# Linear attention and a mixture of adapters on one core: one order of tokens up to the store, x added by several engines, a tangent for the last slots

## The chip, the core and the metric

The kernel runs on one core of a Trainium2 chip. A core has five engines that run their own instruction streams: TensorE (PE, matrix products and transposes into PSUM), VectorE (DVE), ScalarE (ACT), GpSimd (POOL, which has no access to PSUM) and SyncE (SP, used here to issue transfers). Sixteen DMA engines move data between DRAM and the on-chip memory SBUF. An engine works through its stream in order and waits on semaphores for the work of others.

The metric is the time of one execution on the device in microseconds, lower is better.

## The reference

Two stages follow each other. The first is linear attention with cosine weights on q, k, v of shape (8, 8, 576, 64): batch, heads, positions, head size. Each relu'd row is taken twice, times the cosine and times the sine of its position's angle.

```python
    def phi(x, c, s):
        r = np.maximum(x, 0.0)
        return np.concatenate([r * c, r * s], axis=-1)
    q_p = phi(q, cos_w, sin_w)
    k_p = phi(k, cos_w, sin_w)
    kv = np.einsum('bhsf,bhsd->bhfd', k_p, v)
    z = np.sum(k_p, axis=2)
    num = np.einsum('bhsf,bhfd->bhsd', q_p, kv)
    den = np.einsum('bhsf,bhf->bhs', q_p, z)[..., None] + 1e-06
    return (num / den).astype(np.float32)
```

Its result, with the heads side by side, is x: 4608 tokens (8 batches of 576) of 512 numbers. The second stage adds a mixture of eight low-rank adapters: a gate chooses two experts per token, and

```python
    logits = x @ w_gate
    ...
            z = x[mask] @ A[e]
            delta[mask] += w[mask, k, None] * (z @ B[e])
    return (x + delta).astype(np.float32)
```

The output is 4608 x 512 in fp32, 9.44 MB; q, k and v are 9.44 MB each.

## The kernel before

**Tiles.** The 576 positions of a batch are written as 64 rows r of 9 positions s, position = 9 r + s. A batch's q, k and v are loaded with partition = (head parity, r), 128 of them, and cast to bf16 on the way (fp32 for batch 0's k and v). A **slot** n (0 to 35) is 128 tokens: two values of s, with 64 rows each. In the tokens of a slot the number j of the s comes first, then r: token = 64 j + r. Slots 4, 13, 22 and 31 are mixed: they take s = 8 of two neighbouring batches. Nine slots make two batches.

**Steps of a batch.** `ldv`, `ldk`, `ldq` load (batch 0's v and k by SP, all others by POOL's queue). `vs` multiplies one s of v by a cosine (i = 0) or a sine (i = 1), on ACT, DVE or POOL; `rk` and `qc` apply relu to k and q; `kv` sums the products of k and v in PSUM, and `kve` copies them out.

**Steps of a slot.** `qt` transposes q; `qe` multiplies it, read from PSUM, by the table `tabq` of cosines and sines into `qT`: 8 columns of 128, half for each table. `nd` gives numerator and denominator (the small constant of the denominator comes in by a product of `ones` and `eps_hi`); `re` and `no` divide, which gives x as a bf16 tile; `xt` and `xe` transpose x; `za` gives the adapters' z and the gate's logits.

**Steps of a group** (three slots, at the end two and one). `mx`, `nm`, `mk`, `tt`, `cb`, `sg` choose the experts and their weights, `zg` weighs z, `zt` transposes it into PSUM, and `ze` copies it to SBUF. Then, for each slot, `dx` (lines 439 and 440) makes the output in PSUM with two products: `turn` times x, and z times B. `oe` copies it into one of 22 output tiles, and `st` stores it.

**Order of tokens.** `turn` is a permutation matrix (line 483): the first product of `dx` adds x and brings its tokens from (j, r) into (r, j). `ze` permutes z in the same way (lines 421 to 423). So the output tile has partition = 2 r + j, and the store walks DRAM as r, j, d:

```python
        t = out.rearrange("(x r s) d -> x s r d", s=NS, r=HALF)
        dst = t[b:b + 2, s] if mixed(n) else t[b, s:s + 2]
        ...
        e.dma_start(out=dst[:, :, c].rearrange("j r d -> r j d"), in_=o_t[n % NO][:, c])
```

One piece is 2 KB, the 512 numbers of a token; a store has 128 of them, 256 KB.

**What sets the order.** The text `ORDER` lists every step with its engine (T, A, V, G or W for POOL, S); each engine's stream is its steps in that order, and no scheduler moves them. W is a POOL step that in addition waits for DVE's last `vs`, `rk` or `qc`. Buffers set waits too: slot n's `oe` takes the tile that slot n - 22 stored from, and most output tiles lie in the memory of batches whose k and v are used up. SP's stream is five loads at the start, then `gate`, then all 36 stores. `gate` (line 219) is a pair of transfers of two elements each: the first reads v of batch 7, and so waits until that load has landed, and the second waits for the first. No store is issued before that.

Of the kernel before, what the change touches and what calls it, by code (L numbers as in the profile page):

```python
# [21 lines left out]
ldv,S,0,0 pre,G start,A ldk,S,0,0 ldw,S ldq,G,0,0 tq,A ldv,G,1,0 ldk,G,1,0 ldq,G,1,0 ldv,G,2,0 vs,A,0,3,0  # L22
vs,V,0,5,1 ldk,G,2,0 cols,V vs,A,0,4,1 vs,V,0,7,1 vs,A,0,5,0 kz,G,1 kz,V,2 vs,A,0,8,0 vs,A,0,8,1 vs,A,0,1,0
vs,V,0,4,0 vs,A,0,7,0 kz,V,0 vs,A,0,0,1 vs,A,0,2,1 vs,A,0,0,0 vs,V,0,6,0 vs,A,0,1,1 vs,A,0,3,1 rk,V,0,0 rk,A,0,1
vs,V,0,2,0 vs,V,0,6,1 kv,T,0,0 qc,V,0,1 kv,T,0,1 qc,V,0,0 kv,T,0,2 qt,T,1 kve,A,0,0 qt,T,0 kve,A,0,1 qe,V,0
cw,A,0 qe,V,1 dm,T,n0 dm,T,n0 dm,T,n0 nd,T,0 qt,T,3 re,V,0 qt,T,2 no,V,0 qe,V,3 vs,G,1,8,0 vs,A,1,3,1 dm,T,b0
dm,T,b0 nd,T,1 vs,A,1,5,0 vs,G,1,6,1 vs,V,1,2,0 xt,T,0 vs,A,1,6,0 vs,W,1,7,1 xe,A,0 re,V,1 qe,V,2 vs,G,1,5,1
vs,A,1,8,1 vs,G,1,0,1 no,V,1 vs,A,1,2,1 ldq,G,2,0 vs,A,1,4,1 vs,V,1,1,1 dm,T,b0 dm,T,b0 dm,T,b0 dm,T,b0 dm,T,b0
dm,T,b0 nd,T,2 vs,V,1,1,0 vs,A,1,0,0 rk,V,1,0 ldv,G,3,0 xt,T,1 vs,A,1,7,0 xe,A,1 vs,V,1,4,0 ldk,G,3,0 dm,T,b0
kv,T,1,0 vs,V,1,3,0 re,V,2 za,T,0 no,V,2 ldq,G,3,0 kv,T,1,1 mx,V,0 nd,T,3 qc,V,1,0 xt,T,2 kv,T,1,2 re,V,3  # L30
qc,V,1,1 xe,A,2 za,T,1 no,V,3 kve,A,1,1 qt,T,4 qt,T,5 kve,A,1,0 za,T,2 qe,V,4 xt,T,3 mx,V,1 xe,A,3 mx,V,2 nd,T,4
qe,V,5 vs,W,2,5,1 vs,A,2,2,0 nm,V,0 mk,V,0 qt,T,6 vs,A,2,8,0 tt,V,0 ldv,G,4,0 re,V,4 cb,V,0 no,V,4 sg,A,0
vs,A,2,2,1 ldk,G,4,0 zg,V,0 cw,A,1 xt,T,4 qt,T,7 qe,V,6 vs,G,2,1,0 vs,A,2,0,1 zt,T,0 nd,T,5 vs,G,2,6,0 ze,A,0
qe,V,7 za,T,3 xe,A,4 vs,G,2,5,0 dx,T,1,b0 re,V,5 mx,V,3 vs,A,2,6,1 vs,G,2,7,0 no,V,5 dx,T,0,b1 vs,A,2,0,0
vs,G,2,4,0 qt,T,8 rk,V,2,0 oe,A,0 nd,T,6 ldq,G,4,0 oe,A,1 xt,T,5 qe,V,8 za,T,4 vs,W,2,1,1 xe,A,5 re,V,6
vs,G,2,3,1 vs,A,2,3,0 mx,V,4 kv,T,2,0 no,V,6 ldv,G,5,0 vs,A,2,7,1 za,T,5 qc,V,2,1 vs,A,2,4,1 nd,T,7 mx,V,5
vs,A,2,8,1 qc,V,2,0 xt,T,6 mk,V,1 kv,T,2,1 nm,V,1 re,V,7 xe,A,6 tt,V,1 cb,V,1 no,V,7 kv,T,2,2 sg,A,1 qt,T,9
zg,V,1 kve,A,2,0 nd,T,8 vs,W,3,0,1 qe,V,9 kve,A,2,1 vs,G,3,0,0 xt,T,7 zt,T,1 qt,T,10 vs,G,3,5,0 re,V,8 za,T,6
ze,A,1 no,V,8 qt,T,11 vs,G,3,5,1 xe,A,7 dx,T,2,b0 qe,V,10 vs,G,3,1,1 nd,T,9 oe,A,2 vs,G,3,2,1 qe,V,11 xt,T,8
vs,A,3,2,0 vs,G,3,8,1 za,T,7 dx,T,3,b1 re,V,9 xe,A,8 ldq,G,5,0 mx,V,7 no,V,9 dx,T,4,b0 vs,A,3,1,0 za,T,8  # L40
rk,V,3,0 vs,G,3,6,1 nd,T,10 oe,A,4 oe,A,3 xt,T,9 mx,V,6 mx,V,8 qt,T,12 re,V,10 vs,W,3,4,1 nm,V,2 vs,A,3,3,0
mk,V,2 no,V,10 kv,T,3,0 vs,G,3,3,1 vs,A,3,4,0 qe,V,12 vs,G,3,7,0 xe,A,9 nd,T,11 vs,G,3,8,0 vs,A,3,7,1 tt,V,2
qc,V,3,1 kv,T,3,1 ldk,G,5,0 vs,A,3,6,0 re,V,11 xt,T,10 cb,V,2 qc,V,3,0 kv,T,3,2 sg,A,2 ldv,G,6,0 xe,A,10 no,V,11
qt,T,13 kve,A,3,1 qt,T,14 zg,V,2 ldk,G,6,0 nd,T,12 vs,A,4,1,0 qe,V,14 xt,T,11 kve,A,3,0 vs,W,4,6,1 zt,T,2 za,T,9
qe,V,13 ldv,G,7,0 xe,A,11 za,T,10 re,V,12 dx,T,5,b0 ze,A,2 no,V,12 vs,G,4,8,1 vs,A,4,3,1 za,T,11 dx,T,6,b1
vs,G,4,5,0 vs,A,4,0,0 mx,V,10 mx,V,9 mx,V,11 nd,T,13 vs,G,4,3,0 nm,V,3 oe,A,6 rk,V,4,0 vs,W,4,2,1 oe,A,5 xt,T,12
mk,V,3 qt,T,16 re,V,13 tt,V,3 qt,T,15 vs,G,4,1,1 xe,A,12 no,V,13 dx,T,7,b1 vs,G,4,7,0 vs,A,4,0,1 dx,T,8,b0
cb,V,3 qe,V,15 vs,G,4,5,1 sg,A,3 nd,T,14 oe,A,7 vs,G,4,4,0 zg,V,3 xt,T,13 oe,A,8 vs,G,4,2,0 qt,T,17 re,V,14
zt,T,3 no,V,14 za,T,12 vs,A,4,6,0 vs,G,4,4,1 kv,T,4,0 xe,A,13 mx,V,12 vs,G,4,7,1 qe,V,16 nd,T,15 vs,A,4,8,0
ldq,G,6,0 qc,V,4,0 xt,T,14 kv,T,4,1 re,V,15 qc,V,4,1 xe,A,14 za,T,13 no,V,15 ze,A,3 kv,T,4,2 vs,W,5,5,0  # L50
vs,A,5,1,1 qe,V,17 za,T,14 vs,G,5,2,0 kve,A,4,0 nd,T,16 mx,V,13 mx,V,14 vs,G,5,5,1 kve,A,4,1 xt,T,15 mk,V,4
nm,V,4 qt,T,19 re,V,16 vs,G,5,2,1 tt,V,4 qt,T,18 xe,A,15 no,V,16 dx,T,10,b0 vs,G,5,7,0 vs,A,5,0,0 cb,V,4
dx,T,9,b1 qe,V,18 vs,G,5,3,1 sg,A,4 nd,T,17 vs,G,5,6,0 oe,A,10 zg,V,4 qt,T,20 vs,G,5,0,1 oe,A,9 xt,T,16 re,V,17
zt,T,4 no,V,17 vs,G,5,7,1 za,T,15 dx,T,11,b0 xe,A,16 vs,G,5,3,0 mx,V,15 qe,V,19 nd,T,18 ze,A,4 vs,G,5,4,0
oe,A,11 qc,V,5,0 xt,T,17 vs,G,5,1,0 za,T,16 re,V,18 qe,V,20 xe,A,17 dx,T,12,b1 vs,W,5,6,1 dx,T,13,b0 ldk,G,7,0
no,V,18 qt,T,21 za,T,17 oe,A,12 rk,V,5,0 vs,W,5,8,0 nd,T,19 oe,A,13 xt,T,18 mx,V,17 qc,V,5,1 vs,A,5,4,1
vs,W,5,8,1 kv,T,5,0 mx,V,16 nm,V,5 qt,T,22 mk,V,5 re,V,19 tt,V,5 kv,T,5,1 no,V,19 vs,G,6,2,1 vs,A,6,5,1 xe,A,18
# [466 lines left out]
```

## Time and profile before

| | |
|---|---|
| median of 3 runs | 105.99 us (105.93 to 106.36) |
| the profiled execution | 105.92 us |
| its span, first to last instruction | 104.1 us |
| PE, DVE, ACT, POOL busy | 91.0, 87.3, 82.3, 57.3 us |
| mean granted clock of PE | 0.997 |
| moved by the DMA engines | 25.55 MB in 19225 packets |
| HBM read, written | 28.85 MB, 9.44 MB |

The time contains the span and 1.8 us around it. The page gives the span in 40 slices of 2.6 us; "GB/s" is what the DMA engines wrote in a slice. The loads that cast read two bytes for each one they write, so their figure is half of what is read. Queue q0 holds POOL's transfers, q1 those of SP, q10 that of ACT. A busy PE is not a PE at its peak, since matmuls are pipelined and their ends are modelled.

### The profile page before, as it was taken

The numbers are of one execution on the slowest core, as the hardware profiler recorded it, in microseconds if no ns is written. First come the engines' busy times: TensorE is split into PE (matmuls) and PEld (weight loads), VectorE is DVE, ScalarE is ACT, GpSimd is POOL, SyncE is SP. The second block draws the span as 40 slices with busy tenths as digits, with TensorE's granted clock in tenths as the row PEclk, the third lists the DMA queues.
The fourth block names the chain that finished last, engine by engine and source line by source line (L and its number), as shares of the span: only waits on it lengthen the run. The fifth ranks groups of instructions, "written<-read, shape, count | busy, mean of one in ns | idle before, by whom it ended". The sixth has DMA issues, their size and how long they took to land.

```text
span 104.1 us, 3984 instructions
## 1 busy us (share of the span) xinstructions
PE 91.0 (87%) x1620; PEld 65.7 (63%) x1620; DVE 87.3 (84%) x264; ACT 82.3 (79%) x176; POOL 57.3 (55%) x112
## 2 busy tenths in 40 slices
PE   4999489879794999999999999999999999998810
PEld 1344267457573887867887789688778677665200
DVE  5058769579995999999999999999999999999710
ACT  6969767918899699999899789979984896967820
POOL 6991004960799696997979869998910000000000
PEclk9999999999999999999999999999999999999998
DMA  2999999999999999999999999999999996989992
GB/s 27 364 358 291 216 208 247 208 207 213 203 208 213 204 206 210 208 213 204 208 210 205 208 207 207 210 206 126 188 397 372 349 334 257 376 307 383 381 384 96
DMA packets 19225, 25.55 MB, mean 245 GB/s; under 512 B 2184, under 2 KB 13448, under 8 KB 19208
## 3 DMA queue, kind: packets, MB, share of 16 engines
q0 software_dynamic: 11616, 12.98, 73.8%
q1 hardware_dynamic: 7064, 12.21, 32.8%
q8 instruction: 12, 0.20, 0.7%
q10 hardware_dynamic: 528, 0.13, 0.6%
q14 instruction: 5, 0.04, 0.1%
HBM read 28.85 MB, written 9.44 MB: 368 GB/s over the span
## 4 chain that ended last, share of the span: by engine, by line
PE 53%; DMA 18%; ACT 11%; POOL 9%; issue 2%; DVE 2%; POOLq 0%; ACTq 0%
DMA q<-in_q_dram 18%; PE nd L324 10%; PE big L258 8%; PE xz L349 6%; PE za L358 6%; PE big L439 6%; PE big L440 5%; PE pq L289 5%; POOL vs L244 4%; ACT xT L353 3%; ACT zgT L423 2%; PE nd L313 2%; POOL q L200 2%; PE xz L415 2%; POOL k L200 1%
## 5 line engine op out<-in xcount | busy, mean ns | idle before, releaser
L244 POOL TENSOR_SCALAR vs<-v,tab 128x256 bf16<-128x256 bf16 x78 | 37.9, 501 | 17.8 <-DMA v<-in_v_dram 8.7
L353 ACT COPY xT<-xz 128x512 bf16<-128x512 bf16 x34 | 20.0, 587 | 8.9 <-PE xz L349 8.3
L297 DVE TENSOR_TENSOR qT<-pq,tabq 128x1024 bf16<-128x1024 bf16 x36 | 23.8, 676 | 0.9 <-PE pq L289 0.8
L243 ACT ACTIVATE vs<-v,tab 128x256 bf16<-128x256 bf16 x43 | 20.0, 512 | 0.9 <-DMA v<-in_v_dram 0.6
L343 DVE TENSOR_TENSOR xt<-nd,rden 128x512 bf16<-128x512 f32 x28 | 19.2, 687 | 0.3
L324 PE MATMUL nd<-kvsb,qT 128*128 128x130 bf16 (+1 forms) x256 | 19.1, 221 | 0.4 <-DVE qT L297 0.4
L258 PE MATMUL big<-vs,k 64*64 64x130 bf16 x576 | 12.4, 221 | 4.3 <-DVE k L251 2.7
L324 PEld LDWEIGHTS <-qT 128*128 128x128 bf16 (+1 forms) x256 | 13.6, 100 | 2.9 <-issue 1.1
L349 PE MATMUL xz<-ident,xt 128*128 128x128 bf16 x144 | 14.1, 220 | 1.2 <-DVE xt L343 0.7
L358 PE MATMUL za<-AW,xT 128*128 128x136 bf16 x144 | 14.4, 223 | 0.1
L258 PEld LDWEIGHTS <-k 64*64 64x64 bf16 x576 | 9.2, 106 | 7.2 <-DVE k L251 3.5
L289 PE MATMUL pq<-ident,qq 128*128 128x128 bf16 x144 | 13.0, 219 | 0.2 <-DVE qq L282 0.2
L439 PE MATMUL big<-xt,turn 128*128 128x512 bf16 x31 | 11.7, 378 | 0.4 <-ACT k L444 0.3
L349 PEld LDWEIGHTS <-xt 128*128 128x128 bf16 x144 | 10.2, 114 | 2.6 <-DVE xt L343 0.9
L440 PE MATMUL big<-Ball,zgT 128*128 128x512 bf16 x31 | 11.8, 380 | 0.0
L468 PE MATMUL nd<-ones 128*128 128x512 bf16 x36 | 9.4, 427 | 1.5 <-DVE eps_hi L469 1.5
L275 ACT CAST kvsb<-big 64x520 bf16<-64x520 f32 x16 | 9.5, 593 | 1.5 <-PE big L258 1.1
L358 PEld LDWEIGHTS <-xT 128*128 128x128 bf16 x144 | 9.4, 98 | 1.9 <-ACT xT L353 0.8
L289 PEld LDWEIGHTS <-qq 128*128 128x128 bf16 x144 | 9.2, 98 | 1.9 <-DVE qq L282 0.3
L319 PE MATMUL nd<-eps_hi,ones 128*128 128x4 bf16 x56 | 9.5, 169 | 0.1
L282 DVE TENSOR_SCALAR qq<-q 128x1152 bf16<-128x1152 bf16 x16 | 8.1, 513 | 0.8 <-DMA q<-in_q_dram 0.8
L468 PEld LDWEIGHTS <-ones 128*128 128x128 bf16 x36 | 3.8, 108 | 6.6 <-issue 1.9
(81 smaller groups left out, 148.1 us busy)
## 6 DMA issues: line engine op xcount, KB each, us to landing
q<-in_q_dram POOLq DMA_DIRECT2D x8, 576.0 KB, 17.1
v<-in_v_dram POOLq DMA_DIRECT2D x7, 576.0 KB, 17.6
k<-in_k_dram POOLq DMA_DIRECT2D x7, 576.0 KB, 17.0
out_dram<-k SPq DMA_DIRECT2D x10, 256.0 KB, 4.2
out_dram<-v0f SPq DMA_DIRECT2D x8, 256.0 KB, 4.5
out_dram<-k0f SPq DMA_DIRECT2D x8, 256.0 KB, 3.8
out_dram<-v SPq DMA_DIRECT2D x6, 256.0 KB, 3.3
v0f<-in_v_dram SPq DMA_DIRECT2D x1, 1152.0 KB, 5.5
```

The costliest lines, as they stand in the source:

```text
L243: return e.activation(dst, src, AF.Copy, bias=0.0, scale=t)
L244: return e.tensor_scalar(out=dst, in0=src, scalar1=t, scalar2=1.0, op0=ALU.mult, op1=ALU.mult)
L258: e.matmul(out=big[halves[g2], par, gp * 2 * W:(gp + 1) * 2 * W], lhsT=k_b[b][pr, 2 * gp + g2, s, :], rhs=vs_t[b % NV][pr, s, 2 * gp + g2, ...
L289: e.transpose(out=d[:, gp, :, jj, :], in_=q2_t[b % 3][:, gp, s].rearrange("p g d -> p (g d)"), identity=ident)
L297: e.tensor_tensor(out=qT_t[n % NQ], in0=src, in1=tab, op=ALU.mult)
L324: e.matmul(out=nd[pr, par, gp * 2 * W:(gp + 1) * 2 * W], lhsT=qT[:, i, gp * 2 + par, js], rhs=kv_t[b % 3][:, par, gp, i, :], start=False, ...
L343: e.tensor_tensor(out=x.rearrange("p (a t d) -> p t a d", t=2, d=D), in0=nds()[:, :, :, 0:D], in1=rd.rearrange("p (t a) -> p t a", t=2).to ...
L349: e.transpose(out=xz[:, c * 128:(c + 1) * 128], in_=x[:, c], identity=ident)
L353: (e.copy if e is nc.scalar else e.tensor_copy)(xT_t[n % 3], src)
L358: e.matmul(out=zs[:, i, :], lhsT=xT_t[n % 3][:, c, :], rhs=AW[:, c, :], start=(c == 0 and i == 0), stop=(c == DCH - 1), skip_group_check=True)
L439: e.matmul(out=d, lhsT=turn, rhs=x_t[n % NX], start=True, stop=False)
L440: e.matmul(out=d, lhsT=zgT_t[g % 3][:, n - GROUPS[g][0], :], rhs=Ball, start=False, stop=True)
```

## The change

- **One order of tokens.** `turn` is gone, `dx` uses the identity, `ze` is a plain copy (on DVE for groups 8 and 12). Output tiles have partition = 64 j + r, and the store walks DRAM as j, r, d.
- **x added by any engine.** A text `ADD` says for each slot who adds x: PE as before (0), `oe` on DVE (1, slot 30), or a new step `ox` on POOL, which adds x to the output tile after `oe` has copied it (2, twelve slots: 3, 12, 16 to 19, 21, 23 to 27). In slots of kinds 1 and 2 `dx` is one product, z times B.
- **Slots 26 on.** `qT` holds q itself and q times the tangent, in place of q times cosine and sine; numerator and denominator are then both too large by 1/cosine, and the small constant is divided by the cosine as well. The plain half is a copy on ACT (`qe,A,n,0`; slot 27's on DVE), the other a product with the table `tanq` on DVE (`qe,V,n,1`). `ones` is replaced by `esec` in the constant's product for these slots. The table is now kept for pairs of s; tables in fp32 are made first, and `tc`, `tn`, `te`, `tl` derive the bf16 ones, the tangent and `esec` from them.
- **A new ORDER** with these steps. Per engine the counts change thus: `vs` ACT 55 to 65, POOL 78 to 73, DVE 11 to 6; warming matmuls `dm` 12 to 11; all else is as listed above. On POOL's queue the loads keep their order, but for v of batch 7, which goes ahead of k of batch 6 (18th of 22 instead of 19th), and several are issued earlier among POOL's other work, q of batch 7 directly behind k of batch 7. The stores have an order of their own: slots 13, 3, 10, 1, 2, 0, 6, 11, 16, 20, 9, 15, 5, 4, 12, 7, 18, 17, 21, 19, 8, 22, 14, 23, 26, 24, 28, 25, 29, 27, 32, 31, 30, 33, 34, 35.

The core of the diff (`ORDER` left out):

```diff
-    turn = sb("turn", [128, 128])
...
+    NP = NS // 2 + 1
+    posq = sb("posq", [128, NP, 128], mybir.dt.int32)
+    cosq = sb("cosq", [128, NP, 128], FP32)
+    sinq = sb("sinq", [128, NP, 128], FP32)
+    tabq = sb("tabq", [128, 2, NP, 128])
+    tanq = sb("tanq", [128, NP, 128])
+    esec = sb("esec", [128, NP, 128])
...
+ADD = "000200000000200022220202222200100000"
...
+    def tc_(e):
+        copy = e.copy if e is nc.scalar else e.tensor_copy
+        copy(tabq[:, 0], cosq)
+        copy(tabq[:, 1], sinq)
+
+    def tn(e):
+        e.reciprocal(cosq, cosq)
+        e.tensor_tensor(out=tanq, in0=sinq, in1=cosq, op=ALU.mult)
+
+    def te(e):
+        e.activation(esec, cosq, AF.Copy, bias=0.0, scale=EPS)
+
+    def tl(e):
+
+        for pr in (slice(32, 64), slice(96, 128)):
+            e.scalar_tensor_tensor(out=esec[pr], in0=cosq[pr], scalar=EPS, in1=esec[pr],
+                                   op0=ALU.mult, op1=ALU.subtract)
...
-    def qe(e, n):
...
+    def qe(e, n, i=None):
+
+        p, dst = tokens(n)[0][1] // 2, qT_t[n % NQ]
+        src = pq[n % 2][:, 0:512].rearrange("p (a t) -> p a t", a=4)
+        if i is None:
+            src = src.unsqueeze(1).broadcast_to([128, 2, 4, 128])
+            tab = tabq[:, :, p].unsqueeze(2).broadcast_to([128, 2, 4, 128])
+        else:
+            dst = dst[:, i]
+            tab = tanq[:, p].unsqueeze(1).broadcast_to([128, 4, 128])
+        if i == 0:
+            return (e.copy if e is nc.scalar else e.tensor_copy)(dst, src)
+        e.tensor_tensor(out=dst, in0=src, in1=tab, op=ALU.mult)
...
-        e.matmul(out=d, lhsT=turn, rhs=x_t[n % NX], start=True, stop=False)
-        e.matmul(out=d, lhsT=zgT_t[g % 3][:, n - GROUPS[g][0], :], rhs=Ball, start=False, stop=True)
+        by_pe = ADD[n] == "0"
+        if by_pe:
+            e.matmul(out=d, lhsT=ident, rhs=x_t[n % NX], start=True, stop=False)
+        e.matmul(out=d, lhsT=zgT_t[g % 3][:, n - GROUPS[g][0], :], rhs=Ball, start=not by_pe, stop=True)
 
     def oe(e, n, h=None):
...
+        if ADD[n] == "1":
+            return e.tensor_tensor(out=d, in0=s, in1=x_t[n % NX], op=ALU.add)
         (e.copy if e is nc.scalar else e.tensor_copy)(d, s)
+
+    def ox(e, n):
+        return e.tensor_tensor(out=o_t[n % NO], in0=o_t[n % NO], in1=x_t[n % NX], op=ALU.add)
 
     def st(e, n, h=None):
         (b, s), _ = tokens(n)
         t = out.rearrange("(x r s) d -> x s r d", s=NS, r=HALF)
         dst = t[b:b + 2, s] if mixed(n) else t[b, s:s + 2]
         c = slice(0, DM) if h is None else slice(h * DM // 2, (h + 1) * DM // 2)
-        e.dma_start(out=dst[:, :, c].rearrange("j r d -> r j d"), in_=o_t[n % NO][:, c])
+
+        e.dma_start(out=dst[:, :, c], in_=o_t[n % NO][:, c])
```

More of the change, by code (lines that the diff above doesn't have):

```diff
@@ L85 @@
+dx,T,33,b1 sg,A,12 st,S,30 dx,T,34,q1 zg,V,12 oe,A,33 zt,T,12 oe,A,34 ze,V,12 st,S,33 dx,T,35,b0 st,S,34 oe,A,35
+st,S,35
 """
@@ L107, in by_rows, with by_tan @@
     return n >= ROWS and not mixed(n)
+def by_tan(n):
+    return n >= TANS
 @with_exitstack
@@ L305, in nd_ @@
             for g2, pr in enumerate(halves):
-                e.matmul(out=nd[:, g2, D:4 * W:W], lhsT=ones[pr, 0:128], rhs=eps_hi2[pr], start=True,
+                e.matmul(out=nd[:, g2, D:4 * W:W], lhsT=el[pr], rhs=r4[pr], start=True,
                          stop=False, skip_group_check=True)
@@ L318, in nd_ @@
         for par in range(2):
-            e.matmul(out=nd[:, par, D:4 * W:W], lhsT=ones[:, 0:128], rhs=eps_hi, start=True,
+            e.matmul(out=nd[:, par, D:4 * W:W], lhsT=el, rhs=r2, start=True,
                      stop=False, skip_group_check=True)
@@ L433, in dx @@
             for i in range(2):
-                e.matmul(out=h[i], lhsT=turn, rhs=x_t[n % NX][:, i * DM // 2:(i + 1) * DM // 2], start=True, stop=False)
+                e.matmul(out=h[i], lhsT=ident, rhs=x_t[n % NX][:, i * DM // 2:(i + 1) * DM // 2], start=True, stop=False)
             for i in range(2):
```

166 lines of the change are left out of this document (83 added, 83 removed).

## The prediction

> **What bounds the kernel now.** I read the page first: busy shares, then the slices of the transfer rate. In the second fence the columns are start, end, length and the busy time of each engine, then the granted clock, the busy share of the 16 DMA engines (above 1 because packets overlap) and GB/s.
>
> ```profile
> span 104.1 us, 3984 instructions
> PE 91.0 (87%) x1620; PEld 65.7 (63%) x1620; DVE 87.3 (84%) x264; ACT 82.3 (79%) x176; POOL 57.3 (55%) x112
> GB/s 27 364 358 291 216 208 247 208 207 213 203 208 213 204 206 210 208 213 204 208 210 205 208 207 207 210 206 126 188 397 372 349 334 257 376 307 383 381 384 96
> ```
>
> ```profile
> 60.00:70.00 10.00, 9.93 (x235) 8.03 (x234) 9.75 (x31) 8.94 (x21) 9.27 (x20) 1.00 1.21 208
> 70.00:75.00 5.00, 5.00 (x89) 4.08 (x87) 5.00 (x15) 4.71 (x11) 4.56 (x8) 1.00 1.05 152
> 75.00:80.00 5.00, 4.87 (x127) 3.86 (x126) 4.96 (x17) 3.68 (x9) 0.94 (x3) 1.00 1.06 378
> 85.00:90.00 5.00, 5.00 (x93) 3.52 (x92) 4.77 (x16) 3.84 (x9) 0.00 (x0) 1.00 0.80 295
> 95.00:100.00 5.00, 3.83 (x23) 1.48 (x21) 3.50 (x12) 3.44 (x8) 0.00 (x0) 1.00 1.03 383
> 100.00:104.10 4.10, 0.00 (x0) 0.00 (x0) 0.00 (x0) 0.00 (x0) 0.00 (x0) 0.92 0.54 201
> ```
>
> The transfers never rest. From about 18 us to 70 the loads hold a flat 203 to 213 GB/s; from 75 us the stores run at up to 383. DVE (9.75 of 10) and PE (9.93) are full as well, so loads and arithmetic advance side by side, and the last ten microseconds are a queue of stores drained at full rate: 24.6 us of stores (9.44 MB at 383) fit between 75 and 102. So the shape of a store bears on the end directly. When stores may begin is in the SP queue, and what carries them in the page's part on queues and in the list of issues:
>
> ```profile
> 66.37 0.75 SPq L221 DMA_DIRECT2D gone<-v  x1
> 70.85 0.58 SPq L222 DMA_DIRECT2D gone<-gone  x1
> 71.55 0.67 SPq L451 DMA_DIRECT2D out_dram<-v0f  x1
> ```
>
> ```profile
> q0 software_dynamic: 11616, 12.98, 73.8%
> q1 hardware_dynamic: 7064, 12.21, 32.8%
> q10 hardware_dynamic: 528, 0.13, 0.6%
> ...
> q<-in_q_dram POOLq DMA_DIRECT2D x8, 576.0 KB, 17.1
> v<-in_v_dram POOLq DMA_DIRECT2D x7, 576.0 KB, 17.6
> k<-in_k_dram POOLq DMA_DIRECT2D x7, 576.0 KB, 17.0
> out_dram<-k SPq DMA_DIRECT2D x10, 256.0 KB, 4.2
> out_dram<-v0f SPq DMA_DIRECT2D x8, 256.0 KB, 4.5
> out_dram<-k0f SPq DMA_DIRECT2D x8, 256.0 KB, 3.8
> out_dram<-v SPq DMA_DIRECT2D x6, 256.0 KB, 3.3
> v0f<-in_v_dram SPq DMA_DIRECT2D x1, 1152.0 KB, 5.5
> k0f<-in_k_dram SPq DMA_DIRECT2D x1, 1152.0 KB, 10.3
> out_dram<-osb SPq DMA_DIRECT2D x4, 256.0 KB, 4.1
> Bf<-in_moe_B_dram SPq DMA_DIRECT2D x1, 256.0 KB, 15.5
> ...
> Af<-in_moe_A_dram SPq DMA_DIRECT2D x1, 128.0 KB, 13.4
> Wf<-in_moe_w_gate_dram SPq DMA_DIRECT2D x1, 16.0 KB, 13.6
> gone<-v SPq DMA_DIRECT2D x1, 0.0 KB
> gone<-gone SPq DMA_DIRECT2D x1, 0.0 KB
> ```
>
> The packet counts say how many engines carry a transfer. A load on q0 is 128 partitions by 4 runs, 512 pieces; 22 loads make 11264, and 11616 leaves 352, which is 22 times 16: sixteen closing packets for each. On q10 one transfer of 512 pieces leaves 16. On q1 the pieces are 2 x 512 (v0f, k0f), 512 (Af), 128 (Wf), 128 (Bf), 36 x 128 (stores) and 2 x 2 (the two-element gate, an element a piece): 6404. That leaves 660. Forty-one transfers with an outer count of 128, or 64 for the stores (their DRAM side is walked r, j, d), take 16 each, 656; the two gates share the other 4, two each. The only transfers whose outer count is 2 are closed by two engines, not sixteen.
>
> **The change part by part.**
>
> *The store's shape.* It now walks DRAM as j, r, d: outer count 2, then 64 rows of 2 KB. Partition order fixes that order, so the 64 cannot come first. If the outer count sets the engines, as the gate's packets suggest, a store has 2 engines with 64 pieces each. At 383 GB/s the 16 engines carry 23.9 each, so two carry 47.9, and 262144 B take 5.48 us; 36 stores take 197.1. Nor does a lone engine seem to hurry: 295 GB/s at share 0.80 and 383 at 1.03 are 369 and 372 for a full share. From the loads I get a quicker bound: q1 moved 12.21 MB in 32.8% of 16 x 104.1 us, 22.3 GB/s of packet time; with the packet overlap of the load stage (1.21) that is 27.0, and the stores take 174.8. For the slower bound each store's issue (0.67 us above) goes unhidden, 24 us more. I take 197.1, the same packets in the same direction. The other bound, a gain or nothing, is that the number of pieces (128) and not the outer count decides; then a store stays at 16 engines, and this edit costs nothing. The gate has two pieces only, so the trace does not separate these two readings.
>
> The Trainium skill (DMA: Bandwidth & Descriptors, section "Why a DMA increments its semaphore by 16 and not by 1") says the slowest dimension not of size one, on both sides, sets the engine count, the largest number up to 16 that divides both; for 128 and 2 that is 2, always the lowest-numbered engines. The gate's packets agree, and no run here yet shows a large transfer of that shape. The same page's specification of about 27 GiB/s for an engine would make the stores an estimated 163 us; the rows above give 23.9 GB/s.
>
> *When stores begin.* SP's gate waits for the last v load. That load was the 19th issued on POOL's queue and is now the 18th, since k 6 moved behind it. A load lasts 589824 B at 208 GB/s, 2.84 us, so the gate moves from 66.4 to 63.5, the first store's issue (5.2 us later) to 68.7. Bytes of stores appear only from 75 us, 3.4 after 71.55; that gives 72.1. Four loads follow the gate's now, not three, and they end at 63.5 + 11.4 = 74.9, so the two engines still owe 2.8 us of load work then.
>
> *x added elsewhere.* Thirteen of PE's dx matmuls go, and 12 POOL additions (ox) and one on DVE, in oe, come. From the chain and groups:
>
> ```profile
> 37.72 0.22 PE big L440
> ```
>
> ```profile
> L244 POOL TENSOR_SCALAR vs<-v,tab 128x256 bf16<-128x256 bf16 x78 | 37.9, 501 | 17.8 <-DMA v<-in_v_dram 8.7 <-PE nd L324 4.9 <-DVE qq L282 1.4
> L297 DVE TENSOR_TENSOR qT<-pq,tabq 128x1024 bf16<-128x1024 bf16 x36 | 23.8, 676 | 0.9 <-PE pq L289 0.8
> L243 ACT ACTIVATE vs<-v,tab 128x256 bf16<-128x256 bf16 x43 | 20.0, 512 | 0.9 <-DMA v<-in_v_dram 0.6 <-DVE ms L373 0.3
> L353 ACT COPY xT<-xz 128x512 bf16<-128x512 bf16 x34 | 20.0, 587 | 8.9 <-PE xz L349 8.3
> L333 DVE RECIPROCAL rden<-nd 128x8 f32<-128x8 f32 x36 | 7.2, 200 | 0.4 <-PE nd L324 0.2
> L353 DVE COPY xT<-xz 128x512 bf16<-128x512 bf16 x2 | 0.8, 424 | 0.2 <-PE xz L349 0.2
> ```
>
> PE saves 13 x 0.22 = 2.9 us, POOL gains 12 of about 1.0 (twice a vs; up to 2.0 if the second input doubles it) and loses five vs, 2.5 us. Nine of the twelve stand behind POOL's last vs and load, where it is idle.
>
> *q by the tangent.* For ten slots DVE multiplies half as much: between 338 (half of 676) and 676, about 424 by the copy of that size, so nine slots save 2.3 us, while slot 27, both halves on DVE, costs 0.2. ACT takes nine copies, 5.3 us by xT's row, and ten vs, 5.1. At the start DVE gets two copies, a reciprocal and a product of 640 columns two corrections and five fills of a few columns, ACT one copy; one warming matmul (dm) less is 0.2 on PE. The reciprocal is the one without a near row: 8 columns took 200 ns, so 640 lie between the 0.4 us of a plain copy and 16 us at 25 ns a column; I take 3, a few ns a column. DVE loses five vs and the copy into turn there. The smaller ze (plain, two of them on DVE) is within 0.1 us each. POOL issues the last q load beside the last k load instead of some ten slots' work later.
>
> *The sum.* In the profiled execution (105.92 us, its span 104.1, so 1.8 outside; the median of the runs is 105.99) the bytes of 100 to 104.1, 0.82 MB, end at 102.15, 1.95 before the span does. With two engines: 72.1 + 2.8 + 197.1 + 1.95 = 274.0, and 1.8 outside: 275.8 us. All that was gained or lost on PE, DVE, ACT and POOL lies under this queue: slot n waits in oe for the store of slot n - 22, whose tile it takes over, and the latest such wait is slot 30's for store 8, the 21st, ended near 74.9 + 21 x 5.48 = 190; the rest of the arithmetic needs some ten microseconds, and 15 stores, 82 us, still stand behind. Even the 16 us reciprocal would be covered. Without that cover the edits are worth what the first rivals give.
>
> **The rivals.**
>
> *All sixteen engines carry the new store* (pieces decide). Then from 72.1 the loads owe 2.8 us and the stores 24.6: 99.5, + 1.95 + 1.8 = 103.3, provided tiles are ready; DVE's 2.1 us in the last ten slots speaks for that, the stage being at 4.96 of 5. For it: 128 pieces are there to spread. Against: it needs the gate's two to be an accident of its two pieces. This is the one that is not slower.
>
> *Sixteen engines, and ACT becomes the bound.* It holds 8.94 of 10 at 60 to 70 and would get four more vs per ten microseconds (2.0): it overruns by 0.9, twice over some 20 us, and in the last stage nine copies (5.3) meet some 1.2 idle in each of four stretches of 5, 0.5 too much: 105.9 + 1.8 + 0.5 = 108.2 us. It decides once ACT's added work exceeds its idle time there.
>
> *Two engines per store, but another pair each time.* Then eight stores run at once, the rate stays, and only the last store takes 5.5 instead of 0.7 us: some 108 us. Nothing in the trace names an engine, so this stays possible.
>
> **How the numbers follow.** Two fixed engines 0.82: the gate is the only outer count below 16 in the trace and the only one not closed by 16. Sixteen engines and faster 0.09, ACT as the bound 0.04, changing pairs 0.03, effects that cancel 0.02. Runs of one kernel spread by 0.4%, so within 0.5% is about no change. Faster 0.09, same 0.02, slower 0.82 + 0.04 + 0.03 = 0.89. The range comes from the quick and slow bounds of the engine: 275.8 - 22.3 = 253.5 and 275.8 + 24 = 300; I put 248 to 300, as the begin may be some 5 us earlier if the gate opens on less traffic. It holds 0.97 of its case, so 0.8 of all, and leaves the cases near 105 out.
>
> **What the changed profile would show.** If right: GB/s near 48 and a DMA digit of 1 or 2 from 75 us on, stores ended 5.5 us apart, idle ACT before oe released by a store, closing packets on q1 of 5 x 16 + 38 x 2 = 156 in place of 660, and a chain that is mostly out_dram. A rate near 383 after 72 us falsifies it. If the pairs change, the rate is 383 but the landing above 6 us. PE's dx group should show 13 fewer first matmuls, POOL 12 additions, the gate an issue near 63.5.

## The result and the profile after

The changed kernel takes 244.49 us (median of 4 executions, 244.35 to 244.58) against 106.05 of the kernel before (4 executions, 105.93 to 106.36): 2.304 times as long, with an interval of 2.299 to 2.310. The forecast was 275.8 us with a range of 248 to 300, so the sign and the cause came out, and the time lies 3.5 us under the range. Here and below, an execution more than 1.5% above the fastest of the same kernel does not enter a ratio.

The page of the changed kernel, its busy shares and slices:

```profile
span 242.6 us, 3992 instructions
PE 97.3 (40%) x1606; PEld 69.3 (29%) x1606; DVE 93.7 (39%) x271; ACT 89.7 (37%) x195; POOL 70.4 (29%) x119
...
PEclk9988999999999995587555575755555555555555
DMA  6999999999994111111112111112111111211110
GB/s 221 288 224 208 209 207 208 208 208 207 208 213 120 54 53 51 51 54 51 51 51 89 51 51 51 51 51 89 51 51 51 51 51 51 89 51 51 51 51 33
```

Before, 75 us on was the fast end of the kernel, at 295 to 383 GB/s. Now, from the 13th slice on (6.07 us each), the rate is 51 to 54 GB/s, but for the 120 of the crossing, three slices of 89 and the last one. No engine is busy for more than 40% of the span. The rest of the page, the part on queues, tells how many DMA engines close a transfer:

```profile
q0 software_dynamic: 11616, 12.98, 31.3%
q1 hardware_dynamic: 6616, 12.21, 13.8%
```

The load queue is as it was. SP's queue has lost 448 of its 660 closing packets: 6616 - 6404 leaves 212. The SP queue's own issues (start, length, and what is issued) show when the stores begin and at which pace they are taken:

```profile
63.54 0.75 SPq L237 DMA_DIRECT2D gone<-v  x1
68.17 0.57 SPq L238 DMA_DIRECT2D gone<-gone  x1
68.86 0.36 SPq L498 DMA_DIRECT2D out_dram<-v  x1
...
186.32 4.95 SPq L498 DMA_DIRECT2D out_dram<-v0f  x1
191.37 10.00 SPq L498 DMA_DIRECT2D out_dram<-k0f  x2
201.46 16.24 SPq L498 DMA_DIRECT2D out_dram<-k  x4
```

An issue that took 0.67 us now takes 5.0, about the time of one store at 51 GB/s: SP stands in its issues at the pace at which the stores go. The stretches of the same kernel, in the columns of the prediction's second fence:

```profile
72.00:73.00 1.00, 0.93 (x21) 0.66 (x17) 0.98 (x4) 1.00 (x3) 1.00 (x2) 1.00 1.16 254
75.00:76.00 1.00, 1.00 (x31) 0.72 (x30) 1.00 (x3) 0.97 (x4) 0.51 (x2) 1.00 0.28 79
76.00:77.00 1.00, 0.91 (x15) 0.78 (x14) 1.00 (x5) 0.99 (x3) 1.00 (x3) 1.00 0.13 51
130.00:139.00 9.00, 0.00 (x1) 0.00 (x0) 0.00 (x0) 1.51 (x4) 0.85 (x1) 0.50 0.13 51
200.00:230.00 30.00, 0.00 (x0) 0.00 (x0) 0.00 (x0) 0.00 (x0) 0.00 (x0) 0.50 0.15 59
240.00:241.00 1.00, 0.00 (x0) 0.00 (x0) 0.00 (x0) 0.00 (x0) 0.00 (x0) 0.50 0.06 23
241.00:242.60 1.60, 0.00 (x0) 0.00 (x0) 0.00 (x0) 0.00 (x0) 0.00 (x0) 0.50 0.00 0
```

Stores come in at 72 to 73 us (the rate rises from the loads' 208 to 254), the loads end soon after 75, and from 76 on the share of 16 DMA engines is 0.13, which is 2.1 engines. The last bytes go at 240 to 241. From 200 us on no engine computes anything. What the engines wait for (engine, line, waited for; us in total, times, longest):

```profile
ACT k0f L487 <- DMA out_dram<-k0f: 34.7, 2, 29.3
PE xz L391 <- ACT zgT L461: 34.6, 2, 29.4
...
DVE k L486 <- DMA out_dram<-k: 23.2, 1, 23.2
```

`oe` waits for a store that still holds its tile, on ACT and, in slot 30, on DVE, and PE waits behind ACT. The steps that the change added, from the groups (busy, mean ns of one, idle time before):

```profile
L261 DVE RECIPROCAL cosq<-cosq 128x640 f32<-128x640 f32 x1 | 4.1, 4132 | 0.0
L338 DVE TENSOR_TENSOR qT<-pq,tanq 128x512 bf16<-128x512 bf16 x10 | 4.1, 408 | 12.8 <-ACT qT L337 12.8
L337 ACT COPY qT<-pq 128x512 bf16<-128x512 bf16 x9 | 5.3, 593 | 0.1
L490 POOL TENSOR_TENSOR v0f<-v0f,xt 128x512 f32<-128x512 f32 x4 | 4.6, 1154 | 15.8 <-ACT v0f L487 15.4 <-ACT xT L395 0.4
L461 ACT COPY zgT<-xz 128x384 bf16<-128x384 bf16 (+1 forms) x11 | 5.2, 475 | 0.5 <-PE xz L457 0.4
```

### The profile page after: what moved, and what is told of

Its sections match the earlier page's. It is cut to its first block, busy times and chain, and to the rows that moved or that the text cites. A ratio compares the mean times of both kernels' runs of the same rounds, so it can differ in the third digit from the quotient of the medians.

```text
span 242.6 us, 3992 instructions
## 1 busy us (share of the span) xinstructions
PE 97.3 (40%) x1606; PEld 69.3 (29%) x1606; DVE 93.7 (39%) x271; ACT 89.7 (37%) x195; POOL 70.4 (29%) x119
## 3 DMA queue, kind: packets, MB, share of 16 engines
q1 hardware_dynamic: 6616, 12.21, 13.8%
## 4 chain that ended last, share of the span: by engine, by line
DMA 21%; DVE 17%; SPq 16%; PE 12%; ACT 3%; issue 3%; POOL 1%; POOLq 0%; ACTq 0%; DVEq 0%
SPq L498 16%; DMA out_dram<-v0f 8%; DMA out_dram<-k 8%; DMA out_dram<-k0f 6%; DVE xt L385 4%; PE nd L366 3%; DVE qT L338 2%; PE big L291 2%; DVE cosq L261 2%; PE pq L323 1%; PE za L400 1%; PE big L481 1%; PE xz L391 1%; DVE qq L315 1%; DVE k L284 1%
## 5 line engine op out<-in xcount | busy, mean ns | idle before, releaser
L277 POOL TENSOR_SCALAR vs<-v,tab 128x256 bf16<-128x256 bf16 x73 | 36.5, 514 | 16.1 <-DVE m L406 7.3
L391 PE MATMUL xz<-ident,xt 128*128 128x128 bf16 x144 | 15.0, 230 | 34.8 <-ACT zgT L461 34.6
L276 ACT ACTIVATE vs<-v,tab 128x256 bf16<-128x256 bf16 x52 | 24.5, 520 | 0.1
L481 PE MATMUL big<-Ball,zgT 128*128 128x512 bf16 x32 | 13.5, 431 | 12.8 <-ACT v0f L487 12.7
L451 DVE TENSOR_TENSOR zg<-za,u 128x384 bf16<-128x384 f32 (+1 forms) x12 | 6.5, 538 | 29.9 <-ACT u L444 29.9
L338 DVE TENSOR_TENSOR qT<-pq,tabq 128x1024 bf16<-128x1024 bf16 x26 | 17.3, 676 | 1.6 <-PE pq L323 1.6
L487 ACT COPY k0f<-big 128x512 f32<-128x512 f32 x7 | 4.0, 587 | 35.6 <-DMA out_dram<-k0f 34.7
L457 PE MATMUL xz<-ident,zg 128*128 128x128 bf16 x36 | 4.4, 227 | 21.9 <-DVE zg L449 21.9
L490 POOL TENSOR_TENSOR k0f<-k0f,xt 128x512 f32<-128x512 f32 x2 | 2.3, 1154 | 33.0 <-ACT k0f L487 33.0
L515 PE MATMUL nd<-ones 128*128 128x512 bf16 x36 | 10.4, 460 | 1.5 <-DVE eps_hi L516 1.5
```

Source lines behind the costliest of these rows:

```text
L276: return e.activation(dst, src, AF.Copy, bias=0.0, scale=t)
L277: return e.tensor_scalar(out=dst, in0=src, scalar1=t, scalar2=1.0, op0=ALU.mult, op1=ALU.mult)
L338: e.tensor_tensor(out=dst, in0=src, in1=tab, op=ALU.mult)
L391: e.transpose(out=xz[:, c * 128:(c + 1) * 128], in_=x[:, c], identity=ident)
L481: e.matmul(out=d, lhsT=zgT_t[g % 3][:, n - GROUPS[g][0], :], rhs=Ball, start=not by_pe, stop=True)
```

## The experiments

The theory on trial was that the outer count of the store's DRAM side sets the number of DMA engines, and that this alone makes the new time. Rivals were that the other edits have a part in it, and that the number of pieces or the queue, not the outer count, sets the rate.

**The new shape alone.** The kernel before, with the store's walk as its only edit. Output tiles are still in (r, j) order, so the rows of a pair land in each other's places; the time is not touched by that.

```diff
-        e.dma_start(out=dst[:, :, c].rearrange("j r d -> r j d"), in_=o_t[n % NO][:, c])
+        e.dma_start(out=dst[:, :, c], in_=o_t[n % NO][:, c])
```

> The kernel before, with one edit: the store walks DRAM as j, r, d. The output tiles still hold the tokens as r, j, so the two tokens of a pair end up in wrong rows; the work is the same. If the outer count of the store alone makes the change's loss: 32 stores at 51.2 GB/s (5.12 us each, 163.8), four of mixed slots on 16 engines, first bytes near 75 as before, bytes ended near 75 + 1 + 163.8 + 2.5 = 242, so about 246 us, 212 closing packets on q1. If the loss needs the change's other parts (the adds on POOL, the new order, waits of buffers): within a few us of 106.

It took 246.29 us (one execution). Its page:

```profile
GB/s 222 286 224 208 208 208 208 209 209 207 208 166 97 54 51 51 51 54 51 51 51 88 51 51 51 51 51 51 126 51 51 51 51 51 89 51 51 51 51 37
...
q1 hardware_dynamic: 6616, 12.21, 13.6%
```

The same packets, the same 51 GB/s. One line of code makes the whole loss. Under it all else in the change together is worth 1.8 us, less than the 2.9 us by which its first store is issued earlier (68.86 against 71.74).

**Outer counts of 4 and 8.** The kernel before, its stores walking 128 neighbouring rows as 4 x 32 or 8 x 16 (`c=4`, shown here, or `c=8`). Rows land in wrong places; pieces (128 of 2 KB), bytes and queue are unchanged.

```diff
-        e.dma_start(out=dst[:, :, c].rearrange("j r d -> r j d"), in_=o_t[n % NO][:, c])
+        dst = out[n * 128:(n + 1) * 128].rearrange("(i c) d -> c i d", c=4)
+        e.dma_start(out=dst, in_=o_t[n % NO])
```

> The kernel before, every store (mixed slots too) written to 128 neighbouring rows of the output walked as 4 by 32 rows, so the rows are in wrong places; the bytes are the same. If the outer count sets the engines: 4 engines, 102.4 GB/s at 25.6 each, 2.56 us a store, 92 us for 36, so about 75 + 1 + 92 + 4 = 172 us, 6404 + 5 x 16 + 36 x 4 + 4 = 6632 packets on q1. If the rate per engine is the 23.9 GB/s of the full case: 178. If the distance between a store's neighbouring pieces (18 KB in the change, 8 KB here) and not the engines makes it slow: 16 closing packets for each store and a rate that owes nothing to 4/16.

> As the run with 4 by 32 rows, but 8 by 16 (pieces 16 KB apart). If the outer count sets the engines: 8 engines, 1.28 us a store, 46 us, so about 75 + 1 + 46 + 4 = 126 us, 6776 packets on q1, a rate near 200 GB/s. If distance between pieces is what costs: about as slow as the changed kernel, 51 GB/s, since 16 KB is near its 18.

They took 172.05 and 126.58 us (one execution each). SP's queue and a stretch of the store stage, first for 4:

```profile
q1 hardware_dynamic: 6632, 12.21, 19.5%
...
100.00:150.00 50.00, 12.51 (x88) 6.21 (x88) 7.36 (x28) 7.57 (x17) 0.00 (x0) 0.60 0.26 102
```

and for 8:

```profile
q1 hardware_dynamic: 6776, 12.21, 26.8%
...
95.00:120.00 25.00, 11.41 (x88) 5.71 (x88) 7.25 (x28) 6.68 (x16) 0.00 (x0) 0.66 0.53 204
```

Over the 6404 pieces there are 228 and 372 closing packets: 5 x 16 for the loads, 2 x 2 for the gate, and 36 x 4 or 36 x 8 for the stores. The share of 16 engines is 0.26 (4.2 engines) and 0.53 (8.5), and the rate 102 and 204 GB/s. With 51 GB/s for an outer count of 2, each engine carries 25.5, at 2, 4 and 8 alike. So the outer count sets the engines, and 128 pieces in the queue do not help. Another rival was the distance between neighbouring pieces of a store: 18 KB in the changed kernel, 8 KB for a count of 4 and 16 KB for 8. At 16 KB the rate is four times that at 18 KB, so it is not the distance. The Trainium skill (DMA: Bandwidth & Descriptors, section "Why a DMA increments its semaphore by 16 and not by 1") says that the slowest dimension that isn't of size one sets the count, the largest number up to 16 that divides it on both sides; the runs at 2, 4 and 8 agree.

**Each store as two transfers of 64 partitions.** The changed kernel, except that a store that isn't mixed goes out once for each j. A half's outer count is 64.

```diff
-        e.dma_start(out=dst[:, :, c], in_=o_t[n % NO][:, c])
+        if mixed(n):
+            return e.dma_start(out=dst[:, :, c], in_=o_t[n % NO][:, c])
+        for j, pr in enumerate(halves):
+            e.dma_start(out=dst[j, :, c], in_=o_t[n % NO][pr, c])
```

> The changed kernel, but every store of a slot that is not mixed is two transfers, one for each j, 64 partitions to 64 rows. If the outer count made the loss, each half has outer count 64 and 16 engines: the store stage returns to several hundred GB/s, and what is left is what the other edits are worth plus SP's issue time, 68 transfers of 0.45 to 0.67 us, 31 to 46 us from 68.9: 104 to 120 us. If 18 KB steps between pieces were the cause, the halves keep those steps, and the time stays near 244.

122.06 us (120.91 to 122.38), 1.146 times the kernel before (1.139 to 1.153): half as long as the changed kernel, still slower than the kernel before, and above the forecast of 104 to 120. Its queue, a late stretch, and the last issues of SP:

```profile
q1 hardware_dynamic: 7576, 12.21, 37.8%
```

```profile
105.00:110.00 5.00, 0.00 (x0) 0.00 (x0) 0.00 (x0) 0.54 (x1) 0.00 (x0) 0.50 0.89 204
```

```profile
112.75 2.39 SPq L501 DMA_DIRECT2D out_dram<-k  x4
115.23 2.48 SPq L501 DMA_DIRECT2D out_dram<-v  x4
```

The queue has 7576 - 6404 = 1172 closing packets, 5 x 16 + 68 x 16 + 2 x 2, so all sixteen engines take part in each half. They are busy (0.89 of 16) and yet move only 204 GB/s; the kernel before moved 383 at 1.03. The packets themselves take longer: on q1 37.8% of 16 x 120.6 us, 729 us, against 546 before (32.8% of 16 x 104.1) and 536 in the changed kernel (13.8% of 16 x 242.6), for the same 12.21 MB. SP's pace is a second limit at the same height: four issues start 2.48 us before the next four, 0.62 for each 131072 B, or 211 GB/s. An earlier stretch of the same run tells the two apart. SP had issued six halves by 76.91 us, partly under the loads, and issued the next only at 78.27:

```profile
72.40 4.51 SPq L501 DMA_DIRECT2D out_dram<-v0f  x6
78.27 1.11 SPq L501 DMA_DIRECT2D out_dram<-k0f  x2
```

```profile
76.00:78.00 2.00, 2.00 (x31) 1.66 (x29) 2.00 (x7) 1.87 (x5) 2.00 (x4) 1.00 0.96 329
```

The one whole store was issued ahead of all halves, at 68.85, so these are halves alone, and with several of them waiting in the queue the engines moved 329 GB/s. So the shape of a half does not hold the stream at 204; from 78.27 to 117.71 SP issues the other 57 transfers, and at the end its issues, 0.6 us each and not stretched as in the changed kernel, set the pace, as far as this trace tells. Why packets are longer when the halves come one by one, no run shows. The Trainium skill (SBUF — State Buffer, section "Door 1: The DMA port swizzle (why `[64,N]` ≈ `[32,N]`)") says that 64 neighbouring partitions reach only 8 of 16 ports, with an asymptote of about 218 GB/s. The 204 lies below it, but the 329 does not: for several transfers in flight, from both halves of the partitions, it is no bound here.

**Sixteen engines without the new store.** What are the other edits worth? The changed kernel with PE adding x in all slots (no `ox`), `turn` back in `dx`, and whole stores that walk r, j, d. `ze` stays a plain copy, since `zt` now turns z. Tangent, start-up, loads and orders are the change's.

```diff
-ADD = "000200000000200022220202222200100000"
+ADD = "000000000000000000000000000000000000"
...
-            e.transpose(out=xz[:, 512 + i * 128:512 + (i + 1) * 128], in_=zg_t[g % 2][:, i], identity=ident)
+            e.transpose(out=xz[:, 512 + i * 128:512 + (i + 1) * 128], in_=zg_t[g % 2][:, i],
+                        identity=turn if turned(GROUPS[g][i]) else ident)
...
-            e.matmul(out=d, lhsT=ident, rhs=x_t[n % NX], start=True, stop=False)
+            e.matmul(out=d, lhsT=turn if turned(n) else ident, rhs=x_t[n % NX], start=True, stop=False)
...
+        if turned(n):
+            return e.dma_start(out=dst[:, :, c].rearrange("j r d -> r j d"), in_=o_t[n % NO][:, c])
...
```

> The changed kernel with whole stores on 16 engines: turn is back (as the first product of dx, and in the place of the identity when z is transposed, so that ze stays plain), PE adds x for every slot, no ox; mixed slots keep j, r, since their 128 rows lie evenly spaced. Tangent, start and order are the change's. If nothing but the store's shape made the loss: about 103 to 106 us, stores near 380 GB/s from 72 us, 660 closing packets on q1. If the added work on ACT (19 more instructions of some 0.5 us) or the 4.1 us reciprocal at the start binds: 106 to 110, with ACT full from 60 to 95 us.

110.29 us (110.24 to 110.44), 1.036 times the kernel before (1.033 to 1.038), which stood at 106.46 beside it. It lies just above the second forecast, 106 to 110. So even with all sixteen engines these edits lose. DVE's timeline (start, length) has the reciprocals, the one of the start and the first and last of the slots; in this kernel:

```profile
8.51 4.13 DVE L266 RECIPROCAL cosq<-cosq 128x640 f32<-128x640 f32 x1
...
20.14 0.21 DVE L380 RECIPROCAL rden<-nd 128x8 f32<-128x8 f32 x1 [1.23 <-PE nd L371]
...
99.04 0.21 DVE L380 RECIPROCAL rden<-nd 128x8 f32<-128x8 f32 x1
```

and in the kernel before:

```profile
16.02 0.21 DVE L333 RECIPROCAL rden<-nd 128x8 f32<-128x8 f32 x1 [0.16 <-PE nd L324]
...
93.72 0.21 DVE L333 RECIPROCAL rden<-nd 128x8 f32<-128x8 f32 x1
```

Slot 0's division is 4.1 us late, by just the length of the large reciprocal, and the last one 5.3 us: what the start loses is not made good by the nine shorter products. From the first division to the end of the span it is 88.5 us (108.6 - 20.14) against 88.1 before (104.1 - 16.02), so of the 4.5 us between these two executions 4.1 lie ahead of it. ACT, too, stands 3.12 us in that reciprocal (`te` needs its result) with `vs` of batch 0 queued behind it. The end follows the arithmetic, not the stores, as two stretches of this kernel show:

```profile
80.00:85.00 5.00, 4.93 (x141) 3.98 (x143) 4.81 (x18) 4.72 (x11) 0.47 (x2) 1.00 0.35 126
95.00:100.00 5.00, 4.34 (x74) 3.17 (x72) 4.37 (x18) 4.84 (x11) 0.00 (x0) 1.00 0.45 166
```

The stores run dry twice (126 and 166 GB/s) while PE, DVE and ACT are near full.

**The reciprocal by itself, added and taken away.** Once added to the kernel before, at the place where the change has it, with ACT's copy of its result behind it (nothing uses either; a fill of its input ends at 2.1 us, when DVE still waits for v); and once taken out of the kernel of the last experiment, with the tangent products that need it and ACT's nine copies for them, so that all slots take both tables on DVE as before.

```diff
+    def tn(e):
+        e.reciprocal(extra, extra)
+
+    def te(e):
+        e.activation(extra2, extra, AF.Copy, bias=0.0, scale=EPS)
```

> The kernel before with the change's reciprocal added alone: DVE takes the reciprocal of 640 fp32 columns of a tile that nothing else reads, where the change has it among the first vs, and ACT makes its copy of 640 columns behind it, with vs of batch 0 waiting in line. If the 3.5% that remain with whole stores come from the start: the first re some 3 to 4.5 us later than 16.0, and the time 109 to 111. If DVE and ACT have slack at the start that takes it up: within 1 us of 106.

```diff
-ROWS, TANS = 27, 26
+ROWS, TANS = 27, 99
...
     def tn(e):
+        return
...
     def te(e):
+        return
...
     def tl(e):
-
+        return
...
     def qe(e, n, i=None):
 
+        if i == 0:
+            return
+        i = None
```

> The run in which PE adds every x with whole stores, without the tangent: every slot is multiplied by cosine and sine on DVE in one product, and the reciprocal, tangent and corrections at the start are left out; vs, loads and order stay the change's. If the reciprocal at the start cost the 4 us: 105 to 107, with the first re near 16 to 17 us. If ACT's ten more vs or the new order cost them: 109 to 111.

Added to the kernel before, it costs some 3.5 us: 109.29 to 110.17 in three executions against 106.10, 1.033 times (1.027 to 1.038). In the profiled execution, a fourth and the longest (110.96), the first division comes at 21.75 us, 5.7 us later than before, where 3 to 4.5 were expected. Without it and the tangent, the other takes 107.25 us (107.17 to 107.36), 1.010 times the kernel before (1.006 to 1.015) and a little above its forecast of 105 to 107. Its divisions:

```profile
15.84 0.21 DVE L385 RECIPROCAL rden<-nd 128x8 f32<-128x8 f32 x1 [0.27 <-PE nd L376]
...
95.56 0.21 DVE L385 RECIPROCAL rden<-nd 128x8 f32<-128x8 f32 x1
```

Slot 0 is on time again. Of the 3.8 us over the kernel before, 1.15 are left. That rest arises behind the start, since the last division is 1.8 us late and the first is not: it lies in the new order or in the `vs` moved to ACT, and no run separates these. From the first division to the end it is 89.4 us here (105.2 - 15.84) and 88.5 with the tangent, so the tangent gains some 0.9 us there and loses more than 4 ahead of it.

**POOL's additions with half stores.** The same kernel with the change's `ADD` text, so that 13 slots go without PE's product, 12 of them with `ox`. Their tiles stay in (j, r) order, and the unmixed ones among them are stored as halves.

```diff
-ADD = "000000000000000000000000000000000000"
+ADD = "000200000000200022220202222200100000"
```

> As the run in which PE adds every x, but the 13 slots of the change whose x is added by POOL or DVE are added so again and stored as two halves; 23 stores are whole. 49 transfers on SP. If SP's issue (0.6 us each) and not PE was the bound of the run with halves alone: 49 x 0.62 = 30.4 us from 68.9 and 3 to the end, 104 to 107. If half stores are slow in themselves (46 ns more for each of their pieces): 13 x 128 / 16 x 46 ns = 4.8 us of every engine more, 106 to 110. Faster than the run in which PE adds every x only if PE is the bound of the last stage.

115.03 us (113.74 to 115.15), 1.080 times the kernel before (1.077 to 1.083); both forecasts, 104 to 107 and 106 to 110, were missed. PE's 13 products are worth less than what half stores cost. The last division comes earlier here (97.2 us against 99.0), but up to 105 us the stores behind it go at 253 to 257 GB/s:

```profile
95.00:100.00 5.00, 4.55 (x62) 2.91 (x56) 4.71 (x19) 4.03 (x11) 2.71 (x3) 1.00 0.87 257
100.00:105.00 5.00, 2.21 (x12) 0.63 (x10) 1.52 (x7) 2.56 (x6) 0.00 (x0) 1.00 0.91 253
```

In the run in which PE adds every x it is 342 GB/s from 100 us on:

```profile
100.00:104.00 4.00, 3.46 (x21) 1.58 (x22) 3.17 (x15) 2.66 (x8) 0.00 (x0) 1.00 0.92 342
```

SP issues 38 of its 49 transfers from 81.2 to 108.5 us almost without a pause, 0.72 us each, where the forecast had 0.62 each from 68.9 us on.

**What can be kept: the plain `ze`.** In the kernel before, `zt` uses `turn` in place of the identity, and `ze` is a plain copy; stores and everything else stay. A second version also issues q of batch 7 directly behind k of batch 7, as the change does.

```diff
             e.transpose(out=xz[:, 512 + i * 128:512 + (i + 1) * 128], in_=zg_t[g % 2][:, i],
-                        identity=ident)
+                        identity=turn)
...
-        src = xz[:, 512:512 + n * 128].rearrange("p (c j r) -> p c j r", c=n, j=2)
-        dst = zgT_t[g % 3][:, 0:n].rearrange("p c (r j) -> p c j r", j=2)
-        (e.copy if e is nc.scalar else e.tensor_copy)(dst, src)
+        (e.copy if e is nc.scalar else e.tensor_copy)(
+            zgT_t[g % 3][:, 0:n], xz[:, 512:512 + n * 128].rearrange("p (c s) -> p c s", c=n))
```

> The kernel before with one edit: z is transposed with turn in the identity's place, which permutes its tokens on the way, and ze is a plain copy. ze falls from 566 to some 475 ns, 1.2 us of ACT over the whole run. If ACT is not the bound of the kernel before: within 0.5 us of 106. If it is: 105 or less.

> The kernel before with the plain ze of the earlier run, and the load of q for batch 7 issued directly behind that of k for batch 7, as in the change. The gap in the loads near 70 to 75 us (152 GB/s) should close and the loads end near 75 instead of 76.2. If the last stage waits for DMA anywhere: 104.5 to 105.5. If it is bound by the arithmetic of the last slots: as the run with the plain ze alone, 105.7.

The first took 105.72 us against 106.46, 0.994 times (0.991 to 0.998); the second 105.98 against 106.10, 0.999 times (0.996 to 1.001). The second has the same plain `ze` and shows no gain that can be told from no change, so the few tenths of a per cent of the first are not secured. The early load does what it should (243 GB/s from 70 to 75 us, against 152, and 398 from 75 to 80, against 378), and the time stays: this speaks for a last stage bound by arithmetic, in which nobody waits for that load. No version here beats the kernel before by more than 0.9%.

## Why the prediction was right and wrong

**Right: the mechanism, its place and its start.** Two engines carry a store, as read from the gate's closing packets; the shape alone makes 246.29 us. The gate is issued at 63.54 (63.5 was forecast), the first store at 68.86 (68.7), bytes of stores come at 72 to 73 (72.1), and the loads end just behind 75 (74.9). From the last bytes to the end of the span are some 1.7 us (1.95), and 1.8 lie outside it. `oe` waits for stores, and slot 30's for store 8 was the latest, though it ended at 173.4 and not near 190, since two of those 21 stores are mixed and the others take 5.1 us (both below). PE's product with x went from 36 to 23, POOL got 12 additions of 1.15 to 1.23 us (1.0 taken, up to 2.0), the half product took 408 ns (424), ACT's copy 593 (587).

**Wrong: "36 stores take 197.1".** The loads end at 75.2 us in the trace, and the last bytes go between 240 and 241, so 165 to 166 us lie between. The mechanism held; two sizes in this term were off, and both made the stores too slow.

- *The number of slow stores.* Four of the 36 aren't slow. The mixed slots 4, 13, 22 and 31 store to s = 8 of two neighbouring batches, and the batches lie exactly 64 rows' steps apart. Walked j, r, d, that is one even row of 128 places, and such a store has all sixteen engines. The closing packets say so: 5 x 16 for the loads, 4 x 16 for the mixed stores, 32 x 2 for the others and 2 x 2 for the gate make 212, just what is left on q1, where the prediction had 156. In the slices they are the 89s, each a mixed store beside a slow one; the first is in the crossing. I took the outer count from the access as it is written and did not ask for which slots its two outer dimensions run together.
- *The pace of an engine.* 23.9 GB/s was read from 95 to 100 us of the kernel before as the rate of an engine. With 2, 4 or 8 at work it carries 25.5, and a store on two takes 5.1 us, not 5.48. Nor does that hang on how few are at work: in the kernel before, too, sixteen engines moved 406 GB/s, 25.4 each, at 76 to 78 us, when stores had piled up behind the loads. At the end SP issues eight stores in 5.38 us, 0.67 each, which is 390 GB/s: there SP's issues, it seems, and not the engines made the 383.

```profile
76.00:78.00 2.00, 1.87 (x62) 1.63 (x59) 2.00 (x7) 1.65 (x5) 0.00 (x0) 1.00 1.06 406
```

```profile
93.86 2.52 SPq L451 DMA_DIRECT2D out_dram<-k0f  x4
96.48 2.67 SPq L451 DMA_DIRECT2D out_dram<-k  x4
99.24 1.28 SPq L451 DMA_DIRECT2D out_dram<-v  x2
```

My two signs against a faster lone engine (369 and 372 GB/s at full share) were both rows with all sixteen at work, so they could not show it. The quick bound, 27.0, was above the measured rate, and yet its 253.5 us lie above the measured time, since it counted 36 slow stores as well.

The count is worth 3.5 stores of 5.48, 19 us, and the pace 12 us of the 31 that the forecast was too long; with either one mended alone it would have been 257 or 262 us, inside the range. With both the sum closes: 32 x 5.1 is 163.2, and each of the three mixed stores behind the crossing adds an eighth of a slow one, 0.64 us, on the two engines, 1.9 in all: 165.1. Then 75.2 + 165.1 + 1.7 + 1.8 is 243.8, 0.7 us under the measured time. The specification of about 27 GiB/s in the Trainium skill (DMA: Bandwidth & Descriptors, section "Specifications") had given an estimated 163 us for all 36; that comes close only because a rate above the measured 25.5 GB/s met four stores too many.

**Wrong, but hidden: the price of the other edits.** "Even the 16 us reciprocal would be covered" held in the changed kernel, where nothing computes after 200 us. The rivals with sixteen engines had no such cover. I took 3 us for the reciprocal and it is 4.13; above all, the first rival (103.3 us) charged nothing for it, and treated the arithmetic as done in time. The kernel with sixteen engines took 110.29. The second rival, 108.2 with ACT as the bound, was nearer for another reason than the one given: most of the loss goes when the reciprocal and the tangent go (110.29 to 107.25). That run takes ACT's nine copies away too, but the traces decide: 4.1 of the 4.5 us lie ahead of the first division, and from there to the end it is 88.5 us against 88.1. So nearly all of the loss lies in the start and not in ACT's last stage, though ACT is nearly full there (4.84 of 5 at 95 to 100 us). "Pairs that change" fell with the flat 51 GB/s.

**The chain of waits** was to be mostly stores. It names them for 38% (SP's issues 16%, three groups of `out_dram` 22%), and goes on through the slots that waited. That was a loose sign; the rate and the packets were the sharp ones.

## What to carry to other kernels

Before a store's access is rewritten, look at its outermost dimension on both sides, after those that lie evenly have merged: a count of 2 left two DMA engines here, with 128 pieces to spread, and the closing packets of a queue tell the count of each transfer that is in a profile. A rate read from a stretch is an engine's own only if nothing else, such as the issuing of the transfers, sets the pace there. If tokens must stay in an order that gives such an outer count, keep the permutation in a matrix product that is there anyway. A stage that costs nothing under a longer queue has to be priced without it as well, above all at the start, where every later slot inherits the delay.

## What the runs showed that was not expected

- An engine carries 25.5 GB/s of 2 KB stores with 2, 4 or 8 at work, and 25.4 with 16 while stores are queued.
- Half stores from 64 partitions move 329 GB/s while several are queued, and 204 where SP issues them one by one; over the run the queue's packets take a third more time (729 us against 546).
- A reciprocal of 640 fp32 columns on DVE takes 4132 ns, 6.5 ns a column, where a plain cast to bf16 of as many is done in 0.68 us; 8 columns take some 200 ns.
- The plain copy of 384 columns out of PSUM takes ACT 485 ns and the permuted one 600 (the 475 and 566 of the groups mix in smaller ones).
- While PE waits for stores its granted clock falls to 0.50 (0.71 on the mean), and its busy sum rises from 91.0 to 97.3 us with fewer matmuls: under a wait, busy time is not a measure of work.

The rows for the cast and the copies, from the kernel in which PE adds every x (a cast of the table on DVE), from the kernel before (the permuted copy) and from its second version with the plain `ze`:

```profile
7.11 0.68 DVE L262 CAST tabq<-cosq 128x640 bf16<-128x640 f32 x1
```

```profile
L423 ACT COPY zgT<-xz 128x384 bf16<-128x384 bf16 x11 | 6.6, 600 | 0.2 <-PE xz L415 0.2
L421 ACT COPY zgT<-xz 128x384 bf16<-128x384 bf16 x11 | 5.3, 485 | 0.2 <-PE xz L415 0.2
```
